# Attention products in full float32 on 64x64 quarters of the array, with e and v unsplit and a new order

## The chip, the cores and the metric

The kernel runs on one NeuronCore of a Trainium2 chip. The metric is the device time of one execution in microseconds. The kernel before took 562.17 us, the median of three runs (560.41 to 565.18).

## The reference

Attention against pooled keys and values, then a block that rotates, mixes over tokens and mixes over channels:

```python
# q, k, v: (8 batches, 8 heads, 576 tokens, 64), float32
k_p = k.reshape(B, H, 72, 8, D).mean(axis=3)
v_p = v.reshape(B, H, 72, 8, D).mean(axis=3)
scores = (q @ k_p.T) / 8;  attn = softmax(scores)      # per head, 576 x 72
x = concat over heads of attn @ v_p                    # (8, 576, 512)
theta = x @ w_theta;  zr, zi = x * cos(theta), x * sin(theta)
u = x + w_tok_r @ zr + w_tok_i @ zi                    # over tokens
out = u + maximum(u @ w_ch, 0)
```

The moe weights arrive as float64, which the kernel takes as pairs of 32-bit words and converts on chip.

## The kernel before, in words

The work is cut into small generators ("streams"), one per piece: `k`, `K` load and pool the keys, `Q` brings and transposes the queries, `v`, `V` load, pool and prepare the values, `S` are the scores and the softmax of one tile of 128 tokens (the fifth tile has 64), `E` turns the weights e of a group of tiles, `X` multiplies e with v ("attend"), `T` computes theta and the rotation, `Z` and `M` split z and mix over tokens (tile py, line 1031), `F` mixes over channels (tile pf, line 1064). `w`, `W`, `h`, `c` convert, turn and split the weights. A long list of words, SCHEDULE, written out at the top, says which stream takes its next step and on which engine (v, g, a for VectorE, GpSimd, ScalarE) where a step can choose. Every engine gets its instructions in that order and works through them in order.

Wherever a product shall have float32 accuracy from the fast float32r format, both operands are split into a high and a low part and three products are added. Line 1031, 1064 and 943 (theta, tile pt) do that throughout, 128 rows by 128 columns of the array, 288 or 512 columns moving.

In the attention, tokens are taken in two groups per batch, 256 and 320 tokens wide. A head has 72 pooled tokens: 64 "main" ones and 8 "rest" ones. Heads go in pairs c = 0..3, 64 rows each.

- `vals` copies the pooled v of each pair block-diagonally into a 128x128 tile, high part Vh and low part Vl, and builds Vr for the rest rows, 96 rows of high, high and low parts, masked by head.
- `soften` writes the scores of one tile (line 701; the 64-token tile by 64x72 products on the two row halves of the array, line 693), takes maximum, exponent, sum and reciprocal, and writes en. From batch 2 on VectorE transposes en in 32x32 blocks into G (lines 785, 788); `turn` then moves those blocks by DMA into eraw (line 851) and splits them into eh, ev (in place, in eraw) and er. In batches 0 and 1 TensorE transposes.
- `attend(b, m, c)` (line 896) issues four float32r products per head pair: Vh with eh, Vl with eh, Vh with ev, Vr with er, into one PSUM bank of the pool "mm" (four banks). Lines 905 and 907 copy the result out into xT. Batch 0 alone (EXACT = 1) is done unsplit: a float32 product Ve with eh on the full array, and one of 32 rows, Vr with er.
- The pool "s" has two buffers of two banks; scores and the turned weights use it.

A float32 product leaves two matmul records in the trace, a float32r one leaves one.

Of the kernel before, what the change touches and what calls it, by code (L numbers as in the profile page):

```python
# [42 lines left out]
T0.4g T0.3 W2v T0.2a T0.2 c0a T0.2 W2 T0.4 w4.0g T0.3 T0.3 T0.2 T0.3 T0.4 W3 c0 Q1.4 T0.3a c0g c0g T0.4 T0.3 T0.4 T0.3
T0.4 c0g W3a T0.4 T0.3 W4 W3 T0.4 K1 Z0.0g K1a c1a S1.0 c1a W4a W4 c1a S1.0 c1 M0.0.0 W4a W4 Z0.1g Q1.4v c1v Z0.0v c1v
Z0.1v S1.0 M0.1.0 W4a W4 M0.0.0 M0.0.0 k2.2 M0.1.0 c2 W3 M0.1.0 W4a S1.0 c1v W4 S1.0g K2.2v c2a W3a W3 v1.2 M0.0.0
S1.0g S1.1 c2a c2a S1.1 S1.0 S1.1 M0.0.1 c2 S1.0v S1.0 c2g V1v S1.0 M0.0.1 M0.0.1 c2v c3 c2v S1.0a M0.1.1 S1.1 c3a
V1.2v S1.1g S1.1g S1.0 V1g c3a Z0.2a c3v S1.2 S1.2 M0.1.1 M0.1.0 S1.1 V1 v2.2 S1.3 M0.0.1 c3 c3g M0.2.0 c3v M0.2.0
M0.1.1 Z0.2v V1g S1.1a S1.1 M0.2.0 c3v M0.1.0a M0.1.1 Q2.0 S1.2 S1.1 k2.0 S1.1a M0.2.0 S1.4 S1.2 V1g Z0.3g M0.2.1
S1.2a S1.1 Q2.0 X1.0.0 X1.0.0v S1.2v X1.0.2 X1.0.1 X1.0.1a X1.0.3 X1.0.3v M0.2.1 S1.3 Z0.3g S1.2 X1.0.2a T1.0g T1.0g
S1.2a M0.0.1g M0.2.0v K2.0v M0.0.0v M0.2.1 M0.2.1 S1.2 T1.0 Q2.0 M0.2.0g S1.2 S1.3 S1.3 S1.2a S1.4 S1.3g k2.1 S1.3g  # L50
V2.2v T1.0 M0.3.0 M0.3.0 M0.1.1a Q2.1 S1.3 K2.1g S1.2 S1.4 T1.0 M0.3.1 S1.3v S1.3 M0.2.1v M0.0.1v M0.0.0g S1.3 M0.3.1
S1.3a K2 M0.2.1g S1.4 M0.3.0 S1.4g T1.1v k3.2 K2a M0.3.1 S1.3 T1.0 M0.3.0 M0.3.1 S1.4v T1.0 K2 M0.3.1g S1.4 Q2.1 v2.0
T1.0a K2v S1.4v S1.4 T1.1g Q2.1 T1.0 S1.4 T1.0 T1.1 S2.0 T1.0 S1.4a S1.4 V2.0g X1.2.2 T1.1 T1.1 M0.1.1g M0.3.0a v2.1
X1.2.0 X1.2.2a M0.3.1g X1.2.1 M0.1.0g S2.0 X1.2.3 T1.1 T1.1 Q3.0 X1.2.0a X1.2.3v M0.3.0v X1.2.1a T1.1v S2.0 T1.2g
F0.0.1 T1.2v T1.1 X1.2.3g S2.0 K3.2g T1.2 S2.0g T1.1 T1.1 S2.0g S2.1 V2.1v T1.3a Q3.0 T1.2 T1.3g T1.2 F0.0.1 S2.1
F0.0.0 S2.0 F0.0.0 T1.2 T1.3 F0.1.1 T1.4g F0.0.1 T1.2 F0.0.0 F0.1.0 S2.1 k3.0 K3.0g T1.2a S2.1 T1.2 T1.2 T1.2 T1.4v
S2.1g V2a F0.1.0 S2.1v k3.1 F0.2.0 T1.3 T1.3 F0.1.1 S2.2 S2.1 T1.3 T1.3 V2g T1.3v F0.0.1 E2.0 T1.3 S2.2 E2.0 S2.4 T1.3
S2.2 T1.3 S2.2 T1.4 T1.4 K3.1g T1.4 E2.0 F0.2.1 S2.3 T1.4 T1.4 F0.1.1 v3.0 T1.4 F0.2.0 F0.3.1 F0.1.0 F0.3.0 T1.4 Q3.0
Z1.0a Z1.1g F0.3.1 S2.2a F0.2.1 S2.2v E2.0 F0.3.0 K3 S2.3 K3a S2.3 M1.1.0 Z1.1v Z1.0g Q3.1 M1.0.0 E2.0a S2.3 M1.0.0
M1.0.1 M1.0.0 V2 S2.2 V3.0g M1.0.0 M1.0.0a F0.3.1 S2.3v M1.0.1 E2.0a V2g M1.0.1 F0.3.0 M1.1.1 S2.3v E2.0g E2.0g M1.1.0  # L60
S2.4 M1.0.1 M1.1.0 F0.1.1 F0.2.1 V2g Q3.1 v3.2 S2.4 K3 S2.4 S2.3 K3a F0.2.0 F0.3.1 Q3.1 M1.1.1 Z1.3g M1.1.1 S2.4a
M1.0.1a X2.0.0 S2.4g M1.1.0 X2.0.1 S2.4 X2.0.3 X2.0.0a v3.1 X2.0.2 X2.0.1a Z1.2a Z1.3v S3.2 X2.0.3a S3.2 S3.3 X2.0.2a
T2.0g T2.0v M1.3.0 E2.2 S3.2 S3.2 S3.2v M1.1.0v Z1.2g T2.0 T2.0 E2.2 E2.2 M1.2.1 T2.0 T2.1a S3.2v M1.2.1 T2.0 M1.1.1
S3.3 V3.1g M1.1.0v M1.2.1 T2.0 E2.2 M1.2.0 S3.4 M1.2.0 S3.0 V3.2v S3.3 M1.2.1 M1.1.1g S3.3 M1.0.1g M1.3.1 T2.1v S3.2
M1.2.0 M1.2.1v E2.2a E2.2g E2.2g E2.2g S3.3a M1.3.1 S3.3v k4.2 M1.2.0 S3.4 M1.2.0a k4.0 M1.3.1 M1.1.1g K4.2g M1.3.0
X2.2.2 M1.3.1 T2.0a S3.4 M1.3.0 S3.3 F0.2.1 X2.2.2a S3.4 T2.0 S3.4v M1.3.0 X2.2.0 S3.4g M1.2.1g X2.2.3 Q4.0 S3.4
# [71 lines left out]

EARLY, EXACT, V_ON_PE, K_ON_PE, Q_ON_PE, SUMS_ON_ACT = 2, 1, 1, 1, 2, 2
BY_ROWS = 1


@with_exitstack
def tile_attn_moe(
# [13 lines left out]
    P = 128  # L160
# [38 lines left out]
    def pick():  # L199

        return now[0]
# [1043 lines left out]
```

## Time and profile before

| what | us |
|---|---|
| median of three runs | 562.17 |
| the profiled execution, its whole time | 560.23 |
| its span, first to last instruction | 558.4 |
| TensorE busy in the span | 541.2 |
| VectorE, ScalarE, GpSimd busy | 457.6, 331.8, 355.7 |

A busy TensorE counts from the start of a matmul to its modelled end, and matmuls overlap, so this share says that work was under way, not that the array streamed at its peak. How long one of a row of equal matmuls costs is read from the starts of what stands before and behind it. The granted clock averaged 0.993 of full over the span.

### The profile page before, as it was taken

The page shows a single profiled execution, that of the slowest core. Times are in us where ns is not written, and L with a number is a line of the kernel's source. Part 1 is how long each engine was busy: PE and PEld are TensorE (multiplying, and loading weights), DVE is VectorE, ACT ScalarE, POOL GpSimd, SP SyncE. Part 2 cuts the span into 40 slices and gives each one's busy share as a digit, 9 for nine tenths or more (in the row PEclk, how much of TensorE's full clock was granted, in tenths as well). Part 3 has the DMA queues.
Part 4 walks back from the last instruction along what each step waited for, and adds up shares of the span by engine and source line. Part 5 has one row for each costly group of instructions (what it writes and reads, how often), then busy time and mean ns, then how long its engine had stood idle before and what let it go on. Part 6 is the DMA issues. An engine that isn't in the chain of part 4 may idle for free.

```text
span 558.4 us, 11489 instructions
## 1 busy us (share of the span) xinstructions
PE 541.2 (97%) x4031; PEld 511.7 (92%) x4031; DVE 457.6 (82%) x850; ACT 331.8 (59%) x757; POOL 355.7 (64%) x497
## 2 busy tenths in 40 slices
PE   8799889999999999999999999999999999999996
PEld 7666779999999989998999999999999999999996
DVE  2899998999898898798988898989759888567354
ACT  3988889886766876549714677567325576233010
POOL 5445756897578997777969777755915564272230
PEclk9799999999999999999999999999999999999999
DMA  9998313665576786546576584337236420311017
GB/s 272 248 290 203 95 49 79 135 119 112 97 137 132 130 127 101 118 88 111 95 118 129 100 147 76 60 78 120 43 50 103 70 45 1 63 29 22 0 24 127
DMA packets 231802, 57.84 MB, mean 104 GB/s; under 512 B 218689, under 2 KB 220353, under 8 KB 231745
## 3 DMA queue, kind: packets, MB, share of 16 engines
q1 hardware_dynamic: 226768, 56.47, 51.8%
q10 hardware_dynamic: 4976, 0.64, 0.8%
q8 instruction: 32, 0.52, 0.4%
q14 instruction: 26, 0.20, 0.1%
HBM read 37.81 MB, written 9.44 MB: 85 GB/s over the span
## 4 chain that ended last, share of the span: by engine, by line
PE 66%; DVE 15%; ACT 8%; issue 4%; SPq 2%; DMA 2%; POOL 2%; DVEq 0%; POOLq 0%; ACTq 0%
PE py L1031 29%; PE pf L1064 12%; PE pt L943 11%; PE s L701 4%; PE pv L896 4%; PE px L957 2%; SPq L851 1%; PE warm L309 1%; DMA eraw<-G 1%; DVE zl L1015 1%; ACT L756 1%; DVE g L951 1%; DVE wsrc_a L366 1%; PE kpp L548 1%; PE vpp L548 1%
## 5 line engine op out<-in xcount | busy, mean ns | idle before, releaser
L1031 PE MATMUL py<-WTl,zh 128*128 128x288 f32 x576 | 82.8, 289 | 0.0
L1031 PE MATMUL py<-WTh,zh 128*128 128x288 f32 x576 | 81.3, 289 | 0.6 <-POOL zh L207 0.6
L1031 PE MATMUL py<-WTh,zl 128*128 128x288 f32 x576 | 81.2, 289 | 0.6 <-DVE er L819 0.5
L1031 PEld LDWEIGHTS py<-WTh,zl 128*128 128x128 f32 x576 | 74.7, 189 | 1.6 <-PE pe L797 0.7
L1031 PEld LDWEIGHTS py<-WTh,zh 128*128 128x128 f32 x576 | 74.4, 189 | 1.1 <-POOL zh L207 0.8
L1031 PEld LDWEIGHTS py<-WTl,zh 128*128 128x128 f32 x576 | 75.0, 190 | 0.3
L190 POOL TENSOR_TENSOR zl<-z,zh 128x256 fp32r<-128x256 f32 (+2 forms) x68 | 54.3, 829 | 27.3 <-ACT zh L205 14.6
L1041 DVE TENSOR_TENSOR xT<-py,xT 128x288 f32<-128x288 f32 x64 | 28.1, 447 | 28.4 <-PE py L1031 28.2
L949 ACT ACTIVATE g<-pt,c_magic 128x512 f32<-128x512 f32 x35 | 24.0, 685 | 45.4 <-PE pt L943 30.2
L190 POOL TENSOR_TENSOR ul<-xT,uh 128x288 fp32r<-128x288 f32 x40 | 33.2, 846 | 17.6 <-ACT uh L205 13.6
L1064 PE MATMUL pf<-uh,chh 128*128 128x288 f32 x256 | 43.7, 293 | 0.2 <-DVE z L983 0.2
L1064 PE MATMUL pf<-uh,chl 128*128 128x288 f32 x256 | 41.9, 287 | 0.0
L1064 PE MATMUL pf<-ul,chh 128*128 128x288 f32 x256 | 41.9, 286 | 0.0
L701 PE MATMUL s<-kpT,qT 128*128 128x144 f32 x256 | 38.5, 297 | 2.5 <-DVE WTl L435 1.4
L943 PE MATMUL pt<-th,xh 128*128 128x512 f32 x148 | 39.7, 391 | 0.4 <-DVE xT L1071 0.3
L943 PE MATMUL pt<-th,xl 128*128 128x512 f32 x148 | 38.1, 380 | 1.4 <-DVE xl L937 1.4
L701 PEld LDWEIGHTS s<-kpT,qT 128*128 128x128 f32 x256 | 35.0, 198 | 3.4 <-DVE WTl L435 1.6
L943 PE MATMUL pt<-tl,xh 128*128 128x512 f32 x148 | 38.0, 380 | 0.0
L190 POOL TENSOR_TENSOR xl<-xT,xh 128x256 fp32r<-128x256 f32 x40 | 29.6, 760 | 12.0 <-ACT xh L205 7.8
L1064 PEld LDWEIGHTS pf<-uh,chh 128*128 128x128 f32 x256 | 36.0, 190 | 1.0 <-PE pf L1064 0.4
L756 ACT ACTIVATE e_eps<-e_eps 128x576 f32<-128x576 f32 (+1 forms) x30 | 20.5, 685 | 27.5 <-DVE e_eps L752 27.3
L1064 PEld LDWEIGHTS pf<-uh,chl 128*128 128x128 f32 x256 | 35.6, 189 | 0.0
(244 smaller groups left out, 1409.0 us busy)
## 6 DMA issues: line engine op xcount, KB each, us to landing
out_dram<-R SPq DMA_DIRECT2D x112, 72.0 KB, 2.2
kpst<-in_k_dram SPq DMA_DIRECT2D x15, 512.0 KB, 4.2
vpst<-in_v_dram SPq DMA_DIRECT2D x28, 256.0 KB, 3.9
qsst<-in_q_dram SPq DMA_DIRECT2D x96, 72.0 KB, 3.0
eraw<-G SPq DMA_DIRECT2D x96, 60.0 KB, 2.2
eraw<-G SPq DMA_DIRECT2D x96, 40.0 KB, 2.0
WTh_st<-in_moe_w_theta_dram SPq DMA_DIRECT2D x4, 512.0 KB, 7.4
wcraw<-in_moe_w_ch_dram SPq DMA_DIRECT2D x4, 512.0 KB, 3.6
```

The lines of the kernel that those rows point to most:

```text
L190: nc.gpsimd.tensor_tensor(out[:, r], a[:, r], b[:, r], op)
L309: nc.tensor.matmul(p[:, 0:P], ident, ident, start=True, stop=True)
L548: nc.tensor.matmul(main[:, 2 * j : 2 * j + 2, :], ident, st[:, :, D * r : D * r + D], **steps[r])
L701: nc.tensor.matmul(scs[c // 2][:n, 2 * SP * (c % 2) : 2 * SP * (c % 2 + 1)], qT[:, c, t0 : t0 + n], kpT[:, c, :], start=True, stop=True,)
L756: nc.scalar.activation(e[:n], e[:n], AF.Exp, scale=scale)
L896: nc.tensor.matmul(as_written(pv[:, :gn]) if pair else pv[:, :gn], l, by_turns(r) if pair else r, start=i == 0, stop=i == len(terms) - 1,)
L943: nc.tensor.matmul(as_written(pt), l[:, c, :], by_turns(r[:, c, :]), start=i == 0, stop=i == 11)
L949: nc.scalar.activation(halves(g), in_order(pt), AF.Identity, bias=c_magic)
L957: nc.tensor.transpose(px[:, P * c : P * c + P], xT[:, c, o], ident)
L1031: nc.tensor.matmul(as_written(py[:, :n]), l[:, kk, :], by_turns(r[:, kk, t]), start=i == 0, stop=i == 3 * NK - 1,)
L1041: nc.vector.tensor_tensor(halves(u), in_order(py[:, :n]), halves(u), ALU.add)
L1064: nc.tensor.matmul(as_written(pv[:, :n]), l[:, kk, o], by_turns(uhl[r][:, kk, t]), start=i == 0, stop=i == 11,)
```

## The change

All batches now do the attention in float32, unsplit. e is no longer split (eh, er and the low parts go, and with them all of `turn` behind its DMAs), nor is v (`vals` shrinks to one masked Vr; pooled v is used as it is). Eight rest columns per head are written twice, so that en has 640 columns and VectorE turns them with one instruction. `attend` handles all four head pairs of a group at once: eight products of 64 rows and 64 columns, which take the four quarters of the array in turn, and four of 32 rows and 128 columns, one for each row quarter, added to them. They go into both two-bank buffers of the pool "s", and two copies of 512 or 640 columns bring them out, in place of four. The 64-token score tile uses the full array (64x144 outputs) in place of 64x72 products. Pooling sums on VectorE are halving adds now, not one reduction. eraw, pooled v and Vr have two buffers. SCHEDULE is a new list; its first and its changed lines say nothing to a reader and are left out, what they do is shown below the diff.

```diff
-EARLY, EXACT, V_ON_PE, K_ON_PE, Q_ON_PE, SUMS_ON_ACT = 2, 1, 1, 1, 2, 2
+EARLY, V_ON_PE, K_ON_PE, Q_ON_PE, SUMS_ON_ACT = 2, 1, 1, 2, 2
...
     def pool_sum(t, width, dst, fine):
         w = width // 2
         e = pick()
-        if e == "v" and not fine:
-            by_pool = "p (r d) -> p d r" if len(t.shape) == 2 else "p c (r d) -> p c d r"
-            nc.vector.tensor_reduce(dst, t.rearrange(by_pool, d=D), AX.X, ALU.add)
-            return
...
+        vm, vr = pooled["vp", b]
...
+        Vr = work([P, P], F32, "Vr", f"Vr{b}", bufs=2)
+        (nc.vector if on_pe else ENG[pick()]).tensor_tensor(
+            Vr.rearrange("p (h d) -> p h d", h=2),
+            vr.unsqueeze(1).broadcast_to([P, 2, D]),
+            mask.unsqueeze(2).broadcast_to([P, 2, D]),
             ALU.mult,
         )
...
-            nc.vector.transpose(
-                Gv[:n, 0:4, mi, :], en[:n, 0:512].rearrange("p (c k) -> p c k", c=4)
-            )
-            nc.vector.transpose(Gv[:n, 4, mi, 0:64], en[:n, 512:576])
+            nc.vector.transpose(Gv[:n, :, mi, :], en[:n].rearrange("p (c k) -> p c k", c=5))
...
-        raw = f32(ev)
-        copy(pick(), eh[:, :, :gn], raw[:, 0:4, :gn])
-        yield
...
-        ENG[pick()].tensor_tensor(
-            ev[:, 0:4, :gn], raw[:, 0:4, :gn], f32(eh[:, :, :gn]), ALU.subtract
-        )
-        yield
-
-    def attend(b, m, c):
+
+    def attend(b, m):
...
+        ev, vm, Vr, xT = parts[b, g0], pooled["vp", b][0], Vrs[b], xTs[b]
+        pvs = [two_banks([P, 2, 512], f"pv{b}_{g0}_{j}") for j in range(2)]
+        for j in range(2):
+            for c in range(2):
+                for hh in range(2):
+                    r, to = slice(64 * hh, 64 * hh + 64), 64 * (hh ^ c)
+                    nc.tensor.matmul(
+                        pvs[j][to : to + 64, c, :gn], vm[r, 2 * j + c, :], ev[r, 2 * j + c, :gn],
+                        start=True, stop=False,
+                    )
+        for c in range(2):
+            for j in range(2):
+                r = slice(64 * c + 32 * j, 64 * c + 32 * j + 32)
+                nc.tensor.matmul(pvs[j][:, c, :gn], Vr[r, :], ev[r, 4, :gn], start=False, stop=True)
+        yield
+
+        for j in range(2):
+            x, pv = xT[:, 2 * j : 2 * j + 2, g0 : g0 + gn], pvs[j][:, :, :gn]
```

Three places show what the new order does. On TensorE, the first token group of batch 2 (py1 is the mixing of batch 1, s3 are scores of batch 3) stood like this before, in 16 rows of which the first eight are shown:

```order
L1031 MATMUL py1_1_1_2058<-WTh_463,zh1_1_1915 128x288 x9
L896 MATMUL pv2_0_0_2158<-eh2_0_1797,Vh_101 128x256
L896 MATMUL pv2_0_0_2158<-eh2_0_1797,Vl_1076 128x256
L896 MATMUL pv2_0_0_2158<-eraw2_0_1796,Vh_101 128x256
L896 MATMUL pv2_0_0_2158<-er2_0_1798,Vr2_2102 128x256
L896 MATMUL pv2_0_1_2165<-eh2_0_1797,Vh_101 128x256
L896 MATMUL pv2_0_1_2165<-eh2_0_1797,Vl_1076 128x256
L896 MATMUL pv2_0_1_2165<-eraw2_0_1796,Vh_101 128x256
L896 MATMUL pv2_0_1_2165<-er2_0_1798,Vr2_2102 128x256
```

The same group stands on TensorE now, whole, between products of the mixing of batch 1:

```order
L903 MATMUL py1_0_1_1983<-WTh_470,zh1_0_1873 128x288 x9
L552 MATMUL pkr3_2044<-ident_77,kpr3_2023 64x64
L764 MATMUL pv2_0_0_2064<-eraw2_0_1812,vp2_1332 64x256 x4
L764 MATMUL pv2_0_1_2065<-eraw2_0_1812,vp2_1332 64x256 x4
L771 MATMUL pv2_0_0_2064<-eraw2_0_1812,Vr2_1423 128x256
L771 MATMUL pv2_0_1_2065<-eraw2_0_1812,Vr2_1423 128x256
L771 MATMUL pv2_0_0_2064<-eraw2_0_1812,Vr2_1423 128x256
L771 MATMUL pv2_0_1_2065<-eraw2_0_1812,Vr2_1423 128x256
L903 MATMUL py1_0_0_1905<-WTh_470,zl1_0_1874 128x288 x9
```

Sixteen products of the full array became eight of a quarter and four of a row quarter, and the group stands between two blocks of mixing products, as it did before.

On VectorE, the beginning of the program (WTh_st holds words of w_theta, wraw words of the token weights, kpp the pooled keys of batch 0) stood like this before:

```order
L268 MEMSET c_half_92 64x1
L269 MEMSET c_half_92 64x1
L357 TENSOR_SCALAR wsrc_b_120<-wraw0_0_117 128x576
L207 COPY kp0_161<-kpp0_141 128x128
L366 SCALAR_TENSOR_TENSOR wsrc_a_119<-wsrc_a_119,chh_st_108 128x576
L207 COPY kp0_161<-kpp0_141 128x128
```

The beginning of VectorE's program reads like this now:

```order
L257 MEMSET c_half_95 64x1
L258 MEMSET c_half_95 64x1
L334 TENSOR_SCALAR WTh_st_117<-WTh_st_117 128x512
L334 TENSOR_SCALAR wsrc_a_124<-wraw0_0_113 128x576
L339 TENSOR_SCALAR WTl_st_122<-WTh_st_117 128x512
L339 TENSOR_SCALAR wsrc_b_125<-wraw0_0_113 128x576
L197 COPY kp0_143<-kpp0_127 128x128
```

Four conversions of weights stand ahead of the first copy of pooled keys, where one stood.

## Rows read from the trace of the kernel before

**Rows 1.** Busy time of each engine, from the page.

```profile
PE 541.2 (97%) x4031; PEld 511.7 (92%) x4031; DVE 457.6 (82%) x850; ACT 331.8 (59%) x757; POOL 355.7 (64%) x497
```

**Rows 2.** What PE waited for from 80 us to the end: total, times, longest us.

```profile
PE pv L896 <- ACT xT L905: 0.8, 2, 0.5
PE py L1031 <- DVE er L819: 0.5, 1, 0.5
PE pt L943 <- DVE xT L1071: 0.3, 1, 0.3
PE px L957 <- DVE g L951: 0.3, 1, 0.3
PE pf L1064 <- DVE z L983: 0.2, 1, 0.2
PE po L1085 <- DVE xT L1071: 0.2, 1, 0.2
```

**Rows 3.** Busy time by stretch: us, PE, PEld, DVE, ACT, POOL, clock, DMA, GB/s.

```profile
0.00:20.00 20.00, 16.76 (x106) 15.50 (x107) 9.11 (x23) 9.63 (x31) 10.39 (x16) 0.91 0.99 286
20.00:40.00 20.00, 17.78 (x134) 14.47 (x132) 18.27 (x37) 17.87 (x79) 8.94 (x11) 0.91 1.03 248
40.00:60.00 20.00, 18.53 (x97) 13.16 (x98) 19.21 (x30) 17.94 (x43) 13.53 (x16) 1.00 0.79 192
60.00:80.00 20.00, 16.52 (x106) 14.26 (x105) 19.05 (x30) 17.41 (x42) 13.70 (x16) 1.00 0.24 82
```

**Rows 4.** Timeline of PE: start us, us, instructions; the beginning, and where the mixing begins.

```profile
1.35 5.49 PE L309 MATMUL warm<-ident 128*128 128x128 f32 x24 [1.35 <-POOL ident masks.py:199]
6.64 2.37 PE L548 MATMUL kpp<-kpst,ident 128*128 128x128 f32 x16
8.84 1.95 PE L548 MATMUL kpp<-early,ident 128*128 128x128 f32 x16
10.63 0.60 PE L609 MATMUL pq<-ident,qsst 128*128 128x128 f32 x4
...
75.25 2.47 PE L1031 MATMUL py<-WTh,zh 128*128 128x288 f32 x18 [0.56 <-POOL zh L207]
```

**Rows 5.** Timeline of PE, 96 to 100 us.

```profile
96.76 0.72 PE L693 MATMUL s<-kpT,qT 64*64 64x72 f32 x16
97.41 1.37 PE L1031 MATMUL py<-WTh,zl 128*128 128x288 f32 x9
98.62 0.27 PE L896 MATMUL pv<-eh,Vh 128*128 128x256 f32 x1
...
99.96 0.28 PE L896 MATMUL pv<-eh,Vh 128*128 128x256 f32 x1
```

**Rows 6.** Timeline of PE, 206 to 213 us, batch 2's other group.

```profile
208.46 0.30 PE L896 MATMUL pv<-eh,Vh 128*128 128x320 f32 x1
...
210.12 0.40 PE L896 MATMUL pv<-eh,Vh 128*128 128x320 f32 x1
```

**Rows 7.** Chain of work that ended last: start us, us, a row of scores alone on PE.

```profile
210.94 0.98 PE s L701 x8
```

**Rows 8.** Timeline of PE in batch 0's attend, 256 tokens, float32.

```profile
35.96 0.70 PE L896 MATMUL pv<-eh,Ve 128*128 128x256 f32 x2
...
37.21 0.70 PE L896 MATMUL pv<-eh,Ve 128*128 128x256 f32 x2
```

**Rows 9.** What DVE waited for in the first 20 us.

```profile
DVE kp L207 <- PE kpp L548: 4.5, 1, 4.5
```

**Rows 10.** Groups by line: count, busy us, mean ns, idle before and what ended it.

```profile
L471 DVE TENSOR_REDUCE kp<-kpst 128x128 f32<-128x1024 f32 x2 | 3.9, 1964 | 0.0
L471 DVE TENSOR_REDUCE vp<-vpst 128x128 f32<-128x1024 f32 x2 | 3.9, 1960 | 0.0
...
L190 POOL TENSOR_TENSOR eraw<-eraw,eh 128x640 fp32r<-128x640 f32 x8 | 12.3, 1556 | 0.3
...
L905 ACT ACTIVATE xT<-pv 128x320 f32<-128x320 f32 x20 | 8.3, 430 | 6.6 <-PE pv L896 5.0 <-DVE R L1101 1.6
```

More of the change, by code (lines that the diff above doesn't have):

```diff
@@ L531, in pool @@
         if (name, b) not in pooled:
-            pooled[name, b] = [work([P, NC, D], F32, name, f"{name}{b}"), None]
+            pooled[name, b] = [work([P, NC, D], F32, name, f"{name}{b}", bufs=2 if name == "vp" else 1), None]
         if j < 2:
@@ L535, in pool @@
         else:
-            dst = pooled[name, b][1] = work([64, D], F32, name + "r", f"{name}r{b}")
+            dst = pooled[name, b][1] = work([st.shape[0], D], F32, name + "r", f"{name}r{b}", bufs=2 if name == "vp" else 1)
         yield from pool_sum(st, POOL * D, dst, b == 0)
@@ L549, in pool_on_pe @@
             else:
-                nc.tensor.matmul(rem, ident[0:64, 0:64], st[:, D * r : D * r + D], **steps[r])
-    Vrs, qTs, parts, er32 = {}, {}, {}, {}
+                n = st.shape[0]
+                nc.tensor.matmul(rem, ident[0:n, 0:n], st[:, D * r : D * r + D], **steps[r])
+    Vrs, qTs, parts = {}, {}, {}
     def keys(b):
@@ L635, in vals @@
-        if "Vl" not in held:
-            held["Vl"] = work([P, NC, P], F32R, "Vl", "Vl")
-            nc.scalar.copy(held["Vl"].rearrange("p c n -> p (c n)"), G[:, 0 : NC * P])
-        Vl = held["Vl"]
-        e = nc.vector if on_pe else ENG[pick()]
-        for hh in range(2):
-            r = slice(64 * hh, 64 * hh + 64)
-            e.tensor_tensor(Vl[r, :, r], vm[r], f32(Vh[r, :, r]), ALU.subtract)
-        yield
-        vrx = work([96, 2, D], F32, "vrx", f"vrx{b}")
-        vrh = work([64, D], F32, "vrh", f"vrh{b}")
@@ L648, in vals @@
-        vr = pooled["vp", b][1]
-        nc.scalar.copy(vrh.bitcast(F32R), vr)
-        for j in range(2):
-            r = slice(32 * j, 32 * j + 32)
-            nc.scalar.copy(vrx[0:32, j], vrh[r])
-            nc.scalar.copy(vrx[32:64, j], vrh[r])
-        yield
-        e = nc.vector if on_pe else ENG[pick()]
-        for j in range(2):
-            r = slice(32 * j, 32 * j + 32)
-            e.tensor_tensor(vrx[64:96, j], vr[r], vrh[r], ALU.subtract)
-        yield
-        Vr = work([96, NC, P], F32R, "Vr", f"Vr{b}")
@@ L661, in vals @@
-        ENG[pick()].tensor_tensor(
-            Vr.rearrange("p (j c) (h d) -> p j (c h) d", j=2, h=2),
-            vrx.unsqueeze(2).broadcast_to([96, 2, 4, D]),
-            mask.rearrange("p c h -> p (c h)").unsqueeze(1).unsqueeze(3).broadcast_to([96, 2, 4, D]),
+        vm, vr = pooled["vp", b]
+        if on_pe:
+            sums = vm
+            vm = pooled["vp", b][0] = work([P, NC, D], F32, "vp", f"vp{b}", bufs=2)
+            copy(pick(), vm, sums)
+            yield
+        Vr = work([P, P], F32, "Vr", f"Vr{b}", bufs=2)
@@ L761, in soften @@
         yield
-        en = temp(b, m, "en", 8 * SP)
+        en = temp(b, m, "en", 8 * (SP + GR))
         if pick() == "a":
@@ L792, in soften @@
             allot(b, g0, nt)
-        eh, ev, er = parts[b, g0]
+        ev = parts[b, g0]
         o = slice(t0 - g0, t0 - g0 + n)
@@ L1143, in A @@
                 stream(f"E{b}.{tiles[0]}", turn(b, tiles[0]))
-            for c in range(NC):
-                stream(f"X{b}.{tiles[0]}.{c}", attend(b, tiles[0], c))
+            stream(f"X{b}.{tiles[0]}", attend(b, tiles[0]))
     def T(b):
```

406 lines of the change are left out of this document (146 added, 260 removed).

## Prediction, made before the changed kernel ran

> **What bounds the kernel now.** I read the page's first part, then what TensorE waited for, then busy time by stretch, and last the timeline of TensorE. TensorE is busy for 541.2 of the 558.4 us of the span, VectorE for 457.6, the others for much less [rows 1]. A busy share can hide waiting, so I looked at the waits: from 80 us to the end TensorE waits for 0.8 + 0.5 + 0.3 + 0.3 + 0.2 + 0.2 = 2.3 us in all [rows 2]. From there on the kernel is as long as its list of matrix products, whatever the other engines do. The first 75 us are another case: TensorE's first mixing product starts at 75.25 us [rows 4], and until then its busy share is 16.5 to 18.5 of 20 us, while VectorE, after an idle beginning (9.11 of 20 us), is busy for 18.3, 19.2 and 19.1 of 20 us [rows 3]. The start is VectorE's. So the sum has two parts: the products that stand behind 75 us, one by one, and whatever moves the start of the mixing.
>
> **The split attend that goes.** In batches 1 to 7 a token group takes 16 float32r products. Twelve of 256 tokens take 99.96 - 98.62 = 1.34 us [rows 5], so 16 take 1.79 us; twelve of 320 tokens take 210.12 - 208.46 = 1.66 us [rows 6], so 16 take 2.21 us. That is 4.0 us a batch. Batch 0 is dearer: one pair of float32 products, one on the full array and one on 32 rows, takes 37.21 - 35.96 = 1.25 us [rows 8].
>
> **What a float32 product costs.** Four score products of 144 columns take 0.98 us in eight records [rows 7], so 0.1225 us a pass of 144 columns, or 0.218 us a pass of 256 and 0.272 us of 320; a product is two passes. The pair of batch 0 has four passes of 256, 0.87 us; the other 0.38 us are the two changes between full array and 32 rows, 0.19 us each. Batch 0's eight pairs are thus about 4 x 1.25 + 4 x (4 x 0.272 + 0.38) = 10.9 us.
>
> **Do tiles of the array run at once?** The 64-token scores of before are eight products of 72 columns that alternate between the two row halves. Sixteen passes of 72 columns, each 0.061 us, would take 0.98 us one after the other; from the first to the next tile's product they take 97.41 - 96.76 = 0.65 us [rows 5], two changes of tile shape included. With 0.08 to 0.19 us for each change, 0.27 to 0.49 us are left, about half of 0.98: both row halves work at the same time. For two column halves in one row half, which the change needs too, the trace has no row. The bounds for its 64x64 products are therefore four at once and two at once. I take four at once, since the quarters use other rows or other output partitions, as the halves do that were seen to overlap; the other end is the first rival.
>
> **The attend that comes.** Per group eight quarter products, 16 passes in four lanes, so 4 x 0.218 = 0.87 us for 256 tokens and 1.09 us for 320; then four products of 32 rows, eight passes in four lanes, so 0.44 and 0.54 us; and three changes of shape, 3 x 0.19 = 0.57 us. Together 1.88 and 2.20 us, 4.08 us a batch, against 4.0. Behind 75 us stand seven batches: +0.6 us. In batch 0 the array saves 10.9 - 4.1 = 6.8 us, all of it in the first 75 us, where it is not the bound.
>
> **The 64-token scores.** Four products of 144 columns now, 0.98 us, where 0.65 us stood: +0.33 us a batch, +2.3 us for the seven behind 75 us. So the saturated part grows by 0.6 + 2.3 = 2.9 us.
>
> **Work that leaves the other engines.** The splitting of e and v goes: for instance 12.3 us of subtractions in 640-wide halves on GpSimd [rows 10], and its like on ScalarE and VectorE; two copies of up to 640 columns replace four of 0.43 us [rows 10]. Behind 80 us the cover for this is the busy TensorE: the whole of it can give back no more than the 2.3 us of waits [rows 2]. Of these the 0.8 us of pv on ScalarE's copies of xT go with the rotation of banks; I take -1 us. The extra DMAs (four more pieces for the rest rows of v, each batch) stand on SP's queue well ahead of the attend that needs them in the new order; I price them at nothing, and if that cover fails an attend waits for one landing of a small piece, which no row here prices.
>
> **The start.** Four things move it.
> VectorE loses four pooling reductions ahead of batch 0's last z, 2 x 1.96 + 2 x 1.96 = 7.8 us [rows 10]. The order puts 24 other instructions there in exchange (109 stood there, 129 do now): halving adds, two conversions of WTh, two more low parts of x. At some 0.45 us each, an estimate below the engine's mean of 457.6 / 850 = 0.54 us [rows 1] since many are small, that is 10.8 us: +3 us net.
> Against that, VectorE waited 4.5 us for the first pooled keys [rows 9], and three more conversions now stand in that hole: -1.5 us.
> The twelve warm-up products, which ran from 1.35 us, are moved to a place behind batch 0's scores. Before, the pooling of keys took 10.63 - 6.64 = 4.0 us right behind them [rows 4]. The warm-up itself took 5.29 us for 24 passes of 128 columns, 0.22 us each, and the second half of the pooling 0.11 us a pass: the lower of TensorE's two clock levels, 1.2 GHz, and the higher. At the lower one the pooling takes up to 4 us more. VectorE has weights to convert meanwhile, so I take +1 us out of 0 to +4.
> Last, TensorE's 6.8 us less. The end that speaks for a gain is all of it, the other is nothing; with VectorE busy over 91% of 20 to 80 us [rows 3] I take a third, rounded up: -2.5 us. And the attention of batch 1 loses its splitting, which in part lies ahead of 75 us on ScalarE and GpSimd: between 0 and -6 us, as much again as TensorE's share; I take -2 us.
> Sum of the start: 3 - 1.5 + 1 - 2.5 - 2 = -2 us, with ends near -8 and +7.
>
> **The sum.** 558.4 + 2.9 - 1 - 2 = 558.3 us of span. The profiled execution took 1.8 us more than its span, so 560.1 us; it is itself 1.9 us below the median of the runs. Where I had to choose in the start I stayed with its slow side, and the tail and the waits lose more work than they gain; I round down to 559 us as the time of a run. That is 0.6% below the median of before. A measurement here tells a change of about 1%, 5.6 us, from none.
>
> **Rivals.**
> First, slower: the quarters work only two at a time. The eight quarter products then take 8 passes in place of 4, +0.87 and +1.09 us, so +1.96 us a batch and, for the seven behind 75 us, +13.7 us: 573 us. It decides from the first saturated attend on, since nothing covers TensorE there. For it speaks that each two neighbours in the list, (rows 0 to 63, outputs 0 to 63) and (rows 64 to 127, outputs 64 to 127), write the same bank, while the halves that were seen to overlap wrote two banks. Against it speaks that they write other partitions of it.
> The Trainium skill, page "TensorEngine Tiling (Array Packing)", section "Restrictions and Gotchas", says that different row tiles write to different PSUM banks and cannot access one bank at the same time. By that rule this rival comes true; the trace agrees only as far as it goes, its one overlapping pair (0.65 us for what would be 0.98 [rows 5]) does use two banks, and no row shows two row tiles in one bank.
> Second, also slower: attend takes both buffers of the pool "s", so scores behind it on TensorE's list wait until two copies of 640 columns have left, each some 0.7 us by the 0.43 us for 320 [rows 10], on engines with lists of their own. In the order a score follows an attend by about 2.5 us of products at the closest, mostly by over 4. If every second of the 14 attends behind 75 us cost 1.5 us, that is 10 us: 569 us.
> Third, faster: the start shrinks by what leaves the three other engines and TensorE together, to its end of -8 us, and the last waits go too: 559 - 6 = 553 us. For it speaks that all of the removed work of batches 0 and 1 was needed before the array could be filled; against it that VectorE, the busiest there, loses nothing by count.
>
> **How the numbers follow.** The forecast, 559 us with 556.6 to 567.8 as its cell: 0.42. The third rival, below 556.6: 0.36. The two slower ones, above 567.8: 0.15 for the first and 0.07 for the second, 0.22. The range from 546 us (the third rival with the start's whole gain, 559 - 8, and another 5 for waits inside the start that no row separates) to 574 us (the first rival at full price) leaves about 2 in 10 out; the forecast's own range is 555 to 564.
>
> **What would show it.** In the profile after: the time from an attend's first product to the next tile's, 1.9 us for 256 tokens and 2.2 us for 320 where I am right, 2.8 and 3.3 us under the first rival. The start of the first mixing product: near 73 us; below 68 us is the third rival. TensorE's waits for ScalarE or VectorE ahead of tile s, some tenths of a microsecond in all, or the second rival. And 0.98 us for the 64-token scores. The prediction is wrong if the saturated part, from the first mixing product to the end, changes by more than 5 us from 483 us.

## The result, and the profile after

| what | before | after |
|---|---|---|
| median of the runs, us | 561.94 (560.41 to 565.18, 4 runs) | 570.23 (569.48 to 573.24, 4 runs) |
| ratio of the medians, 95% interval | | 1.0145 [1.0102, 1.0188] |
| the profiled execution, us | 560.23 | 570.8 |
| its span, us | 558.4 | 569.0 |

The change makes the kernel 8.3 us slower. The two profiled executions lie 10.6 us apart, since that of before was 1.7 us under its median and that of after 0.6 us above; the accounts below are of these two traces, and some 2 us of them are spread between executions.

The page's first part, busy time of each engine (us, share of the span, instructions):

```profile
PE 538.2 (95%) x4095; PEld 495.9 (87%) x4095; DVE 422.5 (74%) x804; ACT 297.8 (52%) x664; POOL 263.0 (46%) x386
```

Against [rows 1] every engine has less to do, GpSimd by 92.7 us and VectorE by 35.1 us, and yet the span is longer. Work that left other engines bought no time here; what counts is where TensorE stands still. Busy time by stretch (us, PE, PEld, DVE, ACT, POOL, granted clock, DMA share, GB/s), to be laid beside [rows 3]:

```profile
0.00:20.00 20.00, 13.15 (x92) 12.11 (x93) 10.07 (x33) 6.92 (x21) 9.63 (x16) 1.00 0.97 272
20.00:40.00 20.00, 11.79 (x77) 9.90 (x75) 19.02 (x38) 19.84 (x97) 9.28 (x9) 0.83 0.90 267
40.00:60.00 20.00, 17.57 (x141) 14.47 (x142) 14.19 (x30) 12.54 (x26) 8.14 (x11) 0.91 0.89 200
60.00:80.00 20.00, 17.39 (x105) 14.82 (x103) 19.32 (x32) 19.02 (x32) 14.04 (x15) 1.00 0.21 53
```

And from the start to the first mixing product, before and after, in the same columns:

```profile
0.00:75.25 75.25, 64.94 (x404) 52.95 (x404) 60.89 (x110) 58.52 (x171) 44.25 (x56) 0.95 0.79 208
0.00:81.26 81.26, 59.90 (x411) 51.30 (x412) 63.86 (x132) 59.57 (x173) 42.30 (x51) 0.94 0.74 200
```

TensorE is busy for 59.9 us of the first 80, before for 69.6. ScalarE is full from 20 to 40 us, and from 40 to 60 us VectorE and ScalarE, which were full there before, have 14.2 and 12.5 us of work. Their longest waits there are for TensorE's list: VectorE waits 2.4 us for a turned weight tile (and 2.1 us for ScalarE's high part of one), ScalarE 2.2 us for pooled v. The timeline of TensorE (start us, us, instructions, in brackets the wait before and its releaser) shows where these stand, and what an attend costs:

```profile
6.18 3.75 PE L528 MATMUL kpp<-kpst,ident 128*128 128x128 f32 x16 [6.18 <-DMA kpst<-in_k_dram]
...
34.29 1.68 PE L409 MATMUL wt<-ident,wsrc_a 128*128 128x128 f32 x8
...
43.20 1.92 PE L409 MATMUL wt<-ident,wsrc_a 128*128 128x128 f32 x8
...
48.96 2.02 PE L528 MATMUL vpp<-early,ident 128*128 128x128 f32 x16 [1.55 <-DMA early<-in_v_dram]
...
52.72 1.09 PE L764 MATMUL pv<-eraw,vp 64*64 64x256 f32 x16
...
81.26 2.47 PE L903 MATMUL py<-WTh,zh 128*128 128x288 f32 x18 [1.81 <-POOL zh L197]
...
112.69 1.09 PE L764 MATMUL pv<-eraw,vp 64*64 64x256 f32 x16
113.71 0.71 PE L771 MATMUL pv<-eraw,Vr 32*128 32x256 f32 x8
114.35 1.37 PE L903 MATMUL py<-WTl,zh 128*128 128x288 f32 x9
...
213.47 1.31 PE L764 MATMUL pv<-eraw,vp 64*64 64x320 f32 x16
214.71 0.82 PE L771 MATMUL pv<-eraw,Vr 32*128 32x320 f32 x8
215.46 0.66 PE L829 MATMUL px<-ident,xT 128*128 128x128 f32 x4
...
427.83 1.19 PE L634 MATMUL s<-kpT,qT 128*64 128x144 f32 x8
428.95 1.37 PE L903 MATMUL py<-WTh,zl 128*128 128x288 f32 x9
```

Batch 0's first attend stands at 52.72 us, behind two turned weight tiles (wt) and the last of its v. Before, it stood at 34.81 us, behind one:

```profile
33.39 1.04 PE L427 MATMUL wt<-ident,wsrc_a 128*128 128x128 f32 x8
...
34.81 0.60 PE L896 MATMUL pv<-eh,Ve 128*128 128x256 f32 x2
```

Between batch 0's scores and this attend, from 24 to 49 us, TensorE now waits six times, 9.9 us in all, the longest 2.5 us for ScalarE and 2.2 us for VectorE; before, it waited for nothing from 24.7 us to its attend. The first mixing product starts at 81.26 us against 75.25 [rows 4]: 6.0 of the 10.6 us. From there to the end it is 569.0 - 81.26 = 487.7 us against 483.1: the other 4.6. What TensorE waited for from 80 us on (total us, times, longest):

```profile
PE py L903 <- POOL zh L197: 1.8, 1, 1.8
PE pv L764 <- DVE e_eps L685: 1.1, 2, 0.9
PE pt L815 <- POOL xh L197: 1.0, 1, 1.0
PE s L634 <- ACT xT L777: 1.0, 1, 1.0
PE px L829 <- DVE xT L913: 0.7, 1, 0.7
PE po L957 <- DVE xT L943: 0.6, 1, 0.6
PE pf L936 <- DVE xT L913: 0.5, 1, 0.5
PE pf L936 <- POOL ul L180: 0.2, 1, 0.2
```

That is 6.9 us where [rows 2] had 2.3. But the first line, 1.8 us, is the wait in front of the first mixing product at 81.26 us, so it is part of the 6.0 us; behind that product 5.1 us are left, +2.8. The attends give back 7 x (4.0 - 1.66 - 1.99) = 2.4 us. A 64-token score tile takes 428.95 - 427.83 = 1.12 us where it took 97.41 - 96.76 = 0.65 [rows 5], so seven cost 3.3 us more (e12 below measures their worth). So 3.7 of the 4.6 us are accounted for, and 0.9 us are not. The clock has no part in it: from 80 to 540 us it is 1.00 in every stretch of 20 us, before and after. Two of the lines are about the pool s: an attend that waits until VectorE has taken the difference of a score tile (e_eps), and a score tile that waits until ScalarE has copied an attend out (xT).

### The profile page after: what moved, and what is told of

Same layout as the page of the kernel before. It is cut to its first block, busy times and chain, and to the rows that moved or that the text cites. A ratio compares the mean times of both kernels' runs of the same rounds, so it can differ in the third digit from the quotient of the medians.

```text
span 569.0 us, 11307 instructions
## 1 busy us (share of the span) xinstructions
PE 538.2 (95%) x4095; PEld 495.9 (87%) x4095; DVE 422.5 (74%) x804; ACT 297.8 (52%) x664; POOL 263.0 (46%) x386
## 4 chain that ended last, share of the span: by engine, by line
PE 63%; DVE 10%; ACT 8%; SPq 7%; DMA 6%; issue 2%; POOL 2%; DVEq 0%; POOLq 0%; ACTq 0%
PE py L903 27%; PE pf L936 12%; PE pt L815 11%; SPq L751 5%; PE s L634 4%; PE pv L764 2%; DMA early<-in_v_dram 2%; PE px L829 2%; PE pv L771 1%; ACT e_eps L677 1%; DMA vprst<-in_v_dram 1%; DVE G L718 1%; DMA eraw<-G 1%; PE kpp L528 1%; DVE sm L691 1%
## 5 line engine op out<-in xcount | busy, mean ns | idle before, releaser
L903 PE MATMUL py<-WTl,zh 128*128 128x288 f32 x576 | 81.5, 287 | 0.0
L180 POOL TENSOR_TENSOR en<-e_eps,ri 128x128 f32<-128x128 f32 (+3 forms) x49 | 26.3, 551 | 78.8 <-DVE ri L693 58.4
L634 PE MATMUL s<-kpT,qT 128*128 128x144 f32 (+1 forms) x320 | 45.9, 289 | 1.9 <-ACT xT L777 1.0
L634 PEld LDWEIGHTS s<-kpT,qT 128*128 128x128 f32 (+1 forms) x320 | 40.7, 179 | 4.3 <-ACT xT L777 1.2
L195 ACT CAST zh<-z 128x1152 fp32r<-128x1152 f32 (+2 forms) x25 | 24.1, 981 | 35.4 <-PE py L903 30.6
L180 POOL TENSOR_TENSOR zl<-z,zh 128x256 fp32r<-128x256 f32 (+2 forms) x48 | 35.9, 782 | 12.6 <-DVE zh L197 8.9
L823 DVE SCALAR_TENSOR_TENSOR g<-g,pt 128x512 f32<-128x512 f32 x35 | 23.7, 678 | 20.7 <-ACT g L821 20.4
L943 DVE SCALAR_TENSOR_TENSOR xT<-pf,xT 128x288 f32<-128x288 f32 x64 | 28.0, 444 | 14.2 <-PE pf L936 14.0
```

What stands on the lines that cost most here:

```text
L180: nc.gpsimd.tensor_tensor(out[:, r], a[:, r], b[:, r], op)
L195: nc.scalar.copy(out, src)
L634: nc.tensor.matmul(scs[c // 2][:n, 2 * SP * (c % 2) : 2 * SP * (c % 2 + 1)], qT[:, c, t0 : t0 + n], kpT[:, c, :], start=True, stop=True,)
L823: nc.vector.scalar_tensor_tensor(halves(g), halves(g), MAGIC, in_order(pt), ALU.subtract, ALU.subtract)
L903: nc.tensor.matmul(as_written(py[:, :n]), l[:, kk, :], by_turns(r[:, kk, t]), start=i == 0, stop=i == 3 * NK - 1,)
L943: nc.vector.scalar_tensor_tensor(halves(oT), in_order(pv[:, :n]), 0.0, halves(oT), ALU.max, ALU.add)
```

## The experiments

Two theories stood at first. A: the code is cheaper, its new order costs the time. B: the code costs it, above all because an attend now needs both buffers of the pool s, which scores and turned weights use too. The old list of words can be given to the new code: words of dropped steps go, and an attend's block and its two copies take the place of the old ones (moved by some words where the pool s would otherwise deadlock).

**e1, e2, e3: the two orders crossed.**

e1 takes the old list throughout, e2 up to the first mixing product and the new one behind it, e3 the other way round. Of e1, the list's beginning and the place of batch 0's first attend (in the new list, then in e1's):

```diff
-w0.0 k0.0 h1 k0.2 k0.1 h1v w0.0v K0.0 Q0.0 h1v
+k0.0 w0.0 w0.0a k0.1 k0.2 D Q0.0 K0.0 w0.0v K0.1
...
-K1 V0a W0 W1v Q1.3 S0.3 w3.1a w2.1a V0 W1 k1.2 S0.3v w3.1v Q1.3a S0.4g w3.0a S0.4 w2.1 X0.0 X0.0a
+Q1.0 S0.4 w1.1v X0.0 X0.0a w1.0g S0.3g X0.0v T0.0g
```

e1: 

> The changed code with the word list of before in the whole program: words of steps that are gone are dropped, and the four products and copies of an attend become its one block of products and two copies, at the place of the old ones. Theory A (the new order costs the time, the code none): the attends save 0.34 us a batch (3.66 against 4.0 us), the 64-token scores cost 0.33 us a batch, so the part from the first mixing product on is again near 483 us, and that product starts at 70 to 76 us: 554 to 562 us. Theory B (the code costs it: an attend now holds both buffers of the pool s, the rest rows of v need four more DMAs a batch): 567 to 573 us, with TensorE's waits behind 80 us again near 7 us.

e2: 

> The changed code with the order of before up to the first mixing product, and the new order from there on. Theory A: the first mixing product starts at 71 to 76 us, where it started at 81.3; the part behind it stays at 488 us; 561 to 566 us. Theory B, or a start that is slow for another reason than its order: it starts at 79 us or later, 568 to 573 us.

e3: 

> The changed code with the new order up to the first mixing product and the order of before from there on. Theory A: the first mixing product stays at 81 us, and what follows shrinks from 488 to 482 to 485 us, TensorE's waits behind 80 us from 6.9 to 2 to 4 us: 564 to 568 us. Theory B: what follows stays at 487 us or more, 569 to 574 us.

Measured: e1 601.18 us (1.0714 [1.0662, 1.0766]), e2 575.65 us (1.0254 [1.0221, 1.0287]), e3 598.08 us (1.0653 [1.0631, 1.0676]). Theory A falls outright: the order of before is the worse one for this code, and by more than B had expected. What TensorE waited for in e1, up to 80 us (first line) and behind:

```profile
PE pv L764 <- DVE WTl L417: 7.6, 2, 4.0
...
PE pv L764 <- DVE e_eps L685: 9.0, 4, 3.8
PE s L634 <- ACT xT L777: 6.2, 10, 0.8
...
PE s L634 <- DVE xT L779: 0.8, 1, 0.8
```

All of these are the pool s. The 7.6 us are batch 0's attends, which wait for VectorE to split the turned weights (WTl) out of the two buffers. The timeline of e1 shows the longest of the others:

```profile
303.45 1.14 PE L634 MATMUL s<-kpT,qT 128*128 128x144 f32 x8
304.53 0.66 PE L764 MATMUL pv<-eraw,vp 64*64 64x256 f32 x8
308.97 1.13 PE L764 MATMUL pv<-eraw,vp 64*64 64x256 f32 x8 [3.78 <-DVE e_eps L685]
310.03 1.24 PE L771 MATMUL pv<-eraw,Vr 32*128 32x256 f32 x8
312.06 2.29 PE L634 MATMUL s<-kpT,qT 128*128 128x144 f32 x8 [0.80 <-DVE xT L779]
```

A score tile takes one buffer, half of the attend the other, and the second half stands for 3.78 us until VectorE has read the scores. Such a wait costs twice: eight score records that took 1.14 us ahead of it take 2.29 behind it, and the stretch shows TensorE at the lower of its clock levels for a part of the time (columns as above):

```profile
300.00:320.00 20.00, 15.42 (x102) 13.38 (x101) 13.52 (x26) 6.53 (x13) 12.41 (x18) 0.74 0.72 130
```

Behind its first mixing product (84.9 us) e1 takes 519.2 us, 36.1 more than before. Waits there are 23.5 against 2.3 us, 21.2 of the 36.1, and 16.0 of the 23.5 are the three lines of the pool s. The four stretches of 20 us below full clock (0.91, 0.91, 0.83, 0.74) lose another 0.61 x 20 = 12.2 us, an estimate that is on the high side, since TensorE stands still for a part of them. The traced execution is the slowest of e1's four (605.94 us). e3, with the same order behind the mixing and another start, takes 516.2 us there.

**e5: is it the pool s in the start?** e2's first mixing product started at 84.97 us, not at 71 to 76, with 7.5 us of waits of pv for WTl. In e5 batch 0's attends take banks of the pool mm instead, one head pair at a time.

```diff
+    def attend_pair(b, m, c):
...
+        pv = bank([P, 512], f"pv{b}_{g0}_{c}")
+        j, cc = c // 2, c % 2
+        for hh in range(2):
+            r, to = slice(64 * hh, 64 * hh + 64), 64 * (hh ^ cc)
+            nc.tensor.matmul(pv[to : to + 64, :gn], vm[r, c, :], ev[r, c, :gn], start=True, stop=False)
+        r = slice(64 * cc + 32 * j, 64 * cc + 32 * j + 32)
+        nc.tensor.matmul(pv[:, :gn], Vr[r, :], ev[r, 4, :gn], start=False, stop=True)
```

> As e2_oldstart, but batch 0's attend works one head pair at a time (two quarter products and one of 32 rows) into one bank of the pool mm each, at the places of before; the other batches attend as changed. Theory E (what broke the old start is the pool s: batch 0's attend waited 7.5 us for both buffers, which the turned weights held): those waits go, the first mixing product starts at 74 to 79 us in place of 85, and with the 488 us behind it the time is 563 to 568 us. Rival F (the start is late for the late v of batch 0 and for the halving adds on VectorE): it still starts at 82 us or later, 572 us or more.

The timelines of TensorE in e2 (first two rows) and in e5:

```profile
44.63 1.85 PE L764 MATMUL pv<-eraw,vp 64*64 64x256 f32 x16 [3.87 <-DVE WTl L417]
...
84.97 1.37 PE L903 MATMUL py<-WTh,zh 128*128 128x288 f32 x9 [0.56 <-POOL zh L197]
```

```profile
34.50 0.65 PE L764 MATMUL pv<-eraw,vp 64*64 64x256 f32 x4
...
76.41 1.37 PE L932 MATMUL py<-WTh,zh 128*128 128x288 f32 x9 [0.56 <-POOL zh L198]
...
80.46 2.53 PE L932 MATMUL py<-WTh,zh 128*128 128x288 f32 x9 [2.68 <-ACT zh L196]
```

Theory E holds for the start: with other banks, and the attend cut into head pairs, the first attend stands at 34.5 us and the mixing starts at 76.4, in the fastest of e5's four executions (569.23 us). But the time missed its range: 571.5 us (1.0177 [1.0147, 1.0208]). At the seam between the two orders TensorE waits 2.7 us for ScalarE, and the granted clock is 0.91 from 80 to 100 us.

**e9, e10, e11: can that start be kept?**

e10 keeps the old list up to batch 1's first attend. e9 moves one word of e5; e11 adds to e9 two letters and the scores of e6:

```diff
-T0.4 K1 Z0.0g K1a c1a S1.0 c1a W4a W4 c1a S1.0 c1 c1 k2.2 c2 c1a Z0.1a Q1.4a M0.0.0
+T0.4 K1 Z0.0g Z0.1a K1a c1a S1.0 c1a W4a W4 c1a S1.0 c1 c1 k2.2 c2 c1a Q1.4a M0.0.0
...
-X3.2g S4.0 T2.3 v4.2 T2.4g
+X3.2v S4.0 T2.3 v4.2 T2.4v
```

e9: 

> As e5_oldstart_mm0, with one word moved: ScalarE's copy of the high part of z for the second output block now stands directly behind GpSimd's for the first, ahead of ScalarE's share of the last weights. In e5 TensorE waited 2.7 us for that copy at the seam between the two orders, and its granted clock fell to 0.91 between 80 and 100 us. Theory E (the rest of e5's loss is that seam): the wait goes and the clock there is 1.00 again, 2.7 + 1.8 = 4.5 us less than e5: 565 to 568 us. Rival (what is gained in the start is always lost behind, because another engine paces the mixing of batch 0): new waits of like size behind 80 us, 569 to 572 us.

e10: 

> As e5_oldstart_mm0, but the order of before is kept for some 100 words more, up to the first attend of batch 1, so that no seam falls in the first mixing. Theory E: as e9, first mixing product at 76 to 77 us, 564 to 568 us. Rival (the new order behind needs its own start): waits at the later seam, 569 us or more.

e11: 

> As e9, and two copies taken from GpSimd to VectorE (the 64-token piece of x of batch 3, and the high part of x of the tile that joins batches 2 and 3, for which TensorE waited 1.0 us), and the 64-token scores on the two row halves again. If each term comes through, 1.0 + 2.3 us less than e9: 562 to 564 us. If the waits of attend and scores for the pool s take the 2.3 us back, as in e6: within 1 us of e9.

Measured: 574.25, 573.38 and 573.45 us (ratios 1.0209, 1.0205, 1.0204, all intervals within 1.016 to 1.025). Theory E missed in all three. The rivals of e10 (569 us or more) and e11 (within 1 us of e9) came in; e9 lies above its rival's range too. The wait at the seam went in e9, but ScalarE, taking z first, was late for the exponents of batch 1 (2.8 us) and for kpT (1.0 us); e10 waited 2.0 us for zh and 3.5 us for e_eps at later places. The first mixing product stood at 81.36, 78.52 and 76.14 us: it varies by some 5 us between e9 and e11, whose starts differ in one score tile alone. e9 and e5 have one and the same order up to the first attend, and it stands at 39.04 us in e9 and at 34.50 in e5: in e9 TensorE waits 2.3 us for the DMA of v and not 0.9, its granted clock from 20 to 40 us is 0.83 and not 0.94, and the pooling of that v takes 3.60 us and not 2.05. The rival that I had set against theory E holds in e10 and e11: the part behind the first mixing product takes 492.8 and 493.6 us there, against 487.7 in the changed kernel, so what is won in this start is lost behind it, at least in orders joined by hand.

**e4, e7, e14: single items of the new start and of the new waits.**

e4 moves the load v0.0, e7 the warm-up D; e14 is e4 with the two letters of e11.

```diff
-h3a v0.1 S0.0 w1.0a
+h3a v0.1 v0.0 S0.0 w1.0a
...
-S0.1a S0.3 v0.0 S0.2v
+S0.1a S0.3 S0.2v
```

```diff
-w0.0 k0.0 h1 k0.2 k0.1 h1v
+w0.0 k0.0 h1 k0.2 k0.1 D h1v
...
-w1.0 w2.1 D Q1.1a
+w1.0 w2.1 Q1.1a
```

e4: 

> The changed kernel with one word moved: the load of the first half of batch 0's v is issued right behind the second half's, ahead of two token weight loads and v of batch 1. Theory C (the late landing of this v at 48.8 us holds TensorE's list and makes the late start): it lands near 40 us, the first attend starts near 46 us in place of 52.7, the first mixing product at 75 to 78 us, 564 to 568 us. Rival D (the softmax of batch 0 on ScalarE sets the start, the v is late beside it): the first mixing product stays at 80 to 82 us, 569 to 573 us.

e7: 

> The changed kernel with the twelve warm-up products at the head of TensorE's list, as before, in place of 35.8 us. Theory G (the late warm-up is what the start lacks): the pooling of the keys takes 4 us in place of 6.8, the first mixing product starts at 78 to 79 us, 567 to 568 us. Rival D (ScalarE's exponents of batch 0, or its late v, set the start whatever the clock): the pooling is faster, the first mixing product stays at 80 to 82 us, 569 to 572 us.

e14: 

> The changed kernel with e4's earlier load of batch 0's v and two copies taken from GpSimd to VectorE (the 64-token piece of x of batch 3 and the high part of x of the tile that joins batches 2 and 3, for which TensorE waited 1.0 us). If single waits of the new order can be taken out one by one: 0.9 us from e4 and 1.0 us, 567.5 to 568.5 us. If they come back elsewhere: 569 to 571 us.

Measured: e4 569.38 us (1.0145 [1.0118, 1.0173]), mixing from 79.48 us; e7 570.46 us (1.0146 [1.0126, 1.0166]), from 80.73; e14 569.65 us (1.0130 [1.0103, 1.0157]), from 80.17. None differs measurably from the changed kernel. In e4 the pooling of that v no longer waits for its DMA, and still the first attend only moves from 52.72 to 50.90 us; in e7 the keys come earlier and TensorE then waits for q and for ScalarE. The new start hangs on no single item. In e14 the 1.0 us of pt for xh stayed: the copies that I moved belong to another tile, so this says nothing on whether that wait can be taken out.

**e6 and e12: the 64-token scores.**

In e6 the changed kernel gets the half-array products back, in e12 the kernel before loses them.

```diff
+            if halves64:
+                for hh in range(2):
+                    r, g = slice(64 * hh, 64 * hh + 64), SP * (hh ^ (c % 2))
+                    nc.tensor.matmul(
+                        scs[hh][:n, SP * c : SP * c + SP],
+                        qT[r, c, t0 : t0 + n],
+                        kpT[r, c, g : g + SP],
...
```

```diff
-        halves = n == 64
+        halves = False
```

e6: 

> The changed kernel with the 64-token scores as products of 64 rows and 72 columns on the two row halves, each half into its own bank, as before (VectorE takes their maximum and difference in two instructions each in place of one). If the tile costs what the prediction said, 0.98 against 0.65 us, the part behind the first mixing product shrinks by 7 x 0.33 = 2.3 us: 567 to 569 us. If waits take it back: 569.5 to 572 us.

e12: 

> The kernel before, with the 64-token scores on the full array (four products of 144 columns in place of eight of 72 on two row halves) and nothing else. If this term is sized rightly, seven tiles behind 75 us cost 0.33 us each where TensorE waits for 2.3 us in all: 2.3 us more, 563.5 to 565 us. If it is hidden, within 0.7 us of before.

e12: 564.24 against 562.26 us, 2.0 us by the medians and 2.2 by the ratio, 1.0039 [1.0021, 1.0058], an interval of 1.2 to 3.3 us. So where TensorE is the bound the term is there in full. The tile itself was priced too low: in e12 too it takes 1.12 us to the next product, not 0.98, so seven should cost 3.3 us, the upper end of the interval. e6: 569.85 us (1.0132 [1.0099, 1.0164]), not measurably less than the changed kernel's 570.23. Its tile is cheaper (0.65 us to the next), but behind 80 us TensorE waits more, by the view of waits:

```profile
PE s L646 <- ACT xT L802: 2.1, 1, 2.1
PE pv L789 <- DVE e_eps L710: 1.8, 2, 1.4
```

The two lines of the pool s grew from 2.1 to 3.9 us, and from 200 to 240 us the granted clock is 0.98 and 0.93, some 1.8 us. This fits a shorter score tile whose gain is lost in a later wait for the same buffers; no run separates that from the clock.

**e8: do the quarters work at once?**

```diff
-        for j in range(2):
-            for c in range(2):
-                for hh in range(2):
+        for c in range(2):
+            for hh in range(2):
+                for j in range(2):
```

> The changed kernel with the eight quarter products of an attend in another order: two on the same quarter in succession, then the next quarter. If four quarters work at once in the changed kernel, a product now waits for the one ahead of it on its quarter, five steps of two passes stand in place of two: 3 x 0.44 = 1.3 us more for 256 tokens and 1.6 us for 320, 2.9 us a batch, 20 us for seven batches: about 590 us. If only two work at once: 5 steps in place of 4, 6 to 7 us more, 577 us. If one at a time: no change, 570 us.

Measured: 574.43 us in one run, 4.2 above the changed kernel. TensorE's timeline, one of the slower attends and a usual one:

```profile
113.71 1.18 PE L764 MATMUL pv<-eraw,vp 64*64 64x256 f32 x16
114.83 0.71 PE L771 MATMUL pv<-eraw,Vr 32*128 32x256 f32 x8
...
501.31 1.11 PE L764 MATMUL pv<-eraw,vp 64*64 64x256 f32 x16
502.35 0.71 PE L771 MATMUL pv<-eraw,Vr 32*128 32x256 f32 x8
```

All three numbers that I had set were wrong. The sixteen passes take 1.12 us in the first, 1.04 in the second and 1.02 in the changed kernel; one after the other they would take 16 x 0.218 = 3.5 us, two at a time 1.74. So four work at once in both orders. Nine of the fourteen attends behind 80 us take only 0.02 us more than in the changed kernel. What was wrong is my assumption that a product whose quarter is busy holds up those behind it. The trace shows nothing of that: even in the slower attend the first four records start at 0, 76, 89 and 106 ns. The 4 us of the whole are not explained, and come from one run.

**e13: one buffer at a time.** What stayed open was whether the waits of e1 are for two buffers at once or for data that the old order brings late.

```diff
-        pvs = [two_banks([P, 2, 512], f"pv{b}_{g0}_{j}") for j in range(2)]
         for j in range(2):
+            pvj = two_banks([P, 2, 512], f"pv{b}_{g0}_{j}")
...
-        for c in range(2):
-            for j in range(2):
+            for c in range(2):
                 r = slice(64 * c + 32 * j, 64 * c + 32 * j + 32)
-                nc.tensor.matmul(pvs[j][:, c, :gn], Vr[r, :], ev[r, 4, :gn], start=False, stop=True)
+                nc.tensor.matmul(pvj[:, c, :gn], Vr[r, :], ev[r, 4, :gn], start=False, stop=True)
+            yield
```

> As e1_oldorder (601 us), but an attend works in two halves of two head pairs, each with one buffer of the pool s, one after the other. TensorE pays for it: the rest products of a half use two row quarters in place of four and there are two more changes of shape, about 0.9 us a group, 12 to 13 us in all behind 80 us. Theory E (what the old order cannot bear is that an attend needs both buffers of s at once): the waits of e1 for the pool go down, pv for WTl in the start from 7.6 to below 4 us, pv for e_eps behind 80 us from 9.0 to below 4, s for xT from 7.0 to below 4, and with them half of the clock's losses: 585 to 595 us. Rival (the old order waits for late data, not for buffers): the waits stay, 608 us or more.

Measured: 597.95 us (1.0619 [1.0578, 1.0660]), 3 us above the range, though below e1. Its attend of 256 tokens takes 111.86 - 109.41 = 2.45 us, 0.8 more, as expected. What TensorE waited for, up to 80 us (two lines) and behind:

```profile
PE pv L765 <- ACT g L837: 4.0, 1, 4.0
PE pv L765 <- DVE WTl L418: 3.1, 1, 3.1
...
PE s L635 <- ACT xT L775: 3.4, 5, 1.0
...
PE s L635 <- DVE xT L777: 0.7, 1, 0.7
```

The 9.0 us of attends waiting for e_eps are gone but for 0.2, scores wait 4.1 us for xT and not 7.0, and only two stretches behind 80 us are below full clock (0.91 each). The part from the first mixing product on shrinks from 519.2 to 596.8 - 83.6 = 513.2 us though its attends cost some 12 us more. So behind 80 us the two buffers were the cause of most of e1's waits: the lines of the pool s fall from 16.0 to 4.3 us, all waits behind the first mixing product from 23.5 to 13.4. The waits that are not for that pool stay, 7.5 us in e1 and 9.1 here. In the start the wait for WTl more than halved, but another of 4.0 us took its place, and the mixing begins at 83.6 us, hardly earlier than in e1; that can be the 3 us of the miss.

## Why the prediction was wrong, point by point

The forecast was 0.6% less time, the measurement is about 1.5% more. The start was to shrink by 2 us and grew by 6.0; the part behind it was to grow by 2.9 - 1 = 1.9 us and grew by 4.6.

- **The split attend that goes; the float32 product; tiles at once.** Right, and on the safe side: 1.66 and 1.99 us where 1.88 and 2.20 were forecast. Four passes of 0.218 and two of 0.218 are 1.31 us, so by estimate the three changes of shape cost some 0.12 us each and not 0.19. The saturated part gains 2.4 us where it should have lost 0.6.
- **The first rival** (two at a time, 573 us) is out, and with it the Trainium skill's rule on row tiles and banks that I had set beside it (page "TensorEngine Tiling (Array Packing)", section "Restrictions and Gotchas"): in this trace two row tiles work in one bank at once, on other partitions of it, for sixteen passes take 1.02 us and not 1.74. The Trainium skill's page "PSUM — Partial Sum Buffer", section "PSUM bank collisions raise a hardware error", ties the collision to a bank and a quadrant of partitions. With that this trace agrees as far as it goes: the row tiles that work at once in one bank share no partition. That the time came out near this rival's is chance.
- **The 64-token scores.** The mechanism was right, the size too small: 0.98 us a tile, read from a row of 128-token scores, where the 64-token tile takes 1.12. That makes +3.3 us where +2.3 was forecast; e12 measures 2.0 to 2.2 us of it.
- **Work that leaves the other engines: -1 us** failed. Behind the first mixing product the waits grew from 2.3 to 5.1 us. Of these 2.1 us are for the pool s, a shared buffer, which less work on the other engines does not free by itself; the other 3.0 us are for single copies and sums of VectorE and GpSimd that come late in the new order, which no run took apart.
- **The start: -2 us** is the step that failed most: it measured +6.0. I added up VectorE's instructions and took VectorE for the bound. The count came out: its busy time up to the first mixing product, before and after, grew from 60.9 to 63.9 us, my +3. But it also stands still for 81.26 - 63.86 = 17.4 us ahead of the mixing, where it stood still for 14.4 and the other terms (-1.5, +1, -2.5, -2) asked for 5 us less. 5.8 of the 17.4 lie between 40 and 60 us, while TensorE comes late to batch 0's attend, at 52.72 us and not at 34.81. The warm-up's +1 is not seen (e7). The -2.5 and -2 of TensorE and the splitting could not be collected, by my reading because that attend had moved. The order showed that: both groups of batch 0 now stand behind two turned weight tiles. I read where instructions stand on VectorE and not where batch 0's attend stands on TensorE. Which of the items ahead of the attend makes it late stays open: the late v alone is not it (e4), nor the late warm-up (e7).
- **The second rival** (the pool s) had the right mechanism, at 0.07 and 569 us, in the wrong place. I looked for scores that wait behind an attend, behind 75 us. The attend itself must wait for both buffers, and in the start the turned weights hold them. In the order of before that costs 7.5 us there and 16.0 us of waits behind it (e1, e2, e13); with the clock's loss, if that is put down to these waits, it is most of the 36 us. The new order has only 2.1 us of such waits behind 80 us, and a late start. That the new order was made for this reason, and that the late start is its price, is my reading; that the old one costs this code far more is measured (e1, 601.18 us).
- **The marks I set** for this: the saturated part changed by 4.6 us, within the 5 us; the first mixing product came at 81 us and not near 73. The range, 546 to 574 us, holds the time.

What stays open: whether some order of the changed code is faster than before. None of the thirteen kernels with the changed code was; the best, e14, e6 and e4, are 1.3 to 1.5% slower than before. And the first attend varies by 4.5 us between executions of the same order (e5, e9), together with the landing of v and the granted clock; each order was traced once, so how often that happens is not known.

## What to carry to other kernels

When a change merges several small blocks of products into one, count the buffers that it needs at the same moment, who else holds them at each place of the program, and how late the last reader is; the saving on the array is small change beside that. In a start-up phase follow the first consumer (here batch 0's attend) in the order of the engine that runs it, ahead of any sum of instructions on another engine. And a wait inside a saturated stretch costs more than its length, since the granted clock may be down behind it.

## What the runs showed of the hardware that was not expected

- The order of 64x64 quarter products hardly matters: with two in succession on one quarter, sixteen passes of 256 columns take 1.04 us in most attends, 1.12 in one of the slower, in place of 1.02 (e8).
- A wait of 3.8 us between products was followed by score blocks at half speed, 2.29 us in place of 1.14, and by a granted clock of 0.74 in that stretch of 20 us (e1); after the 2.7 us at e5's seam it was 0.91.
